# Loading x in single blocks between the gate weights, and x for the residual in four parts along the outputs

## The chip, the cores and the metric

One core of a Trainium2 chip (trn2) runs the whole kernel. The metric is device time in microseconds; the time of a kernel is the median of its runs. Five engines work side by side: TensorE (PE, with its weight loads as PEld), VectorE (DVE), ScalarE (ACT), GpSimd (POOL) and SyncE (SP), whose only work here is to issue DMAs, in the order of its instructions.

## The reference

x is 2048 tokens by 512 channels in bf16. It is normalised once, and two branches are added to it: attention in a sliding window, and a gated MLP that mixes over the tokens.

```python
xn = layernorm(x)
# A: 32 heads of 16 channels, causal, window of 256 keys
q, k, v = split(xn @ wqkv)
p = softmax(mask(q @ k.T * 16 ** -0.5))
A = (p @ v) @ wo
# B: Fh = 688
z = gelu(xn @ w_in)                       # 2048 x 1376
z1, z2 = z[:, :688], layernorm(z[:, 688:])
g = w_sp @ z2 + b_sp[:, None]             # w_sp is 2048 x 2048
B = (z1 * g) @ w_out
out = x + A + B
```

## The kernel before

The tokens are 16 blocks of 128 (`NB`). The work has two stages, and every order in it is written out by hand: each engine runs its instructions in the order in which the program emits them, and SP issues the DMAs in that order too, all on one queue. An instruction that waits holds up everything behind it on its engine.

**Stage one** (to about 56 us) makes, for each block n, the normalised and transposed x and the two gate halves:

- `load_x(n2)` (L189) loads two blocks of x, 2 x 128 rows, with one DMA (L196). Blocks 0 and 1 come as two DMAs (`split`, L194).
- `stats(n)` takes mean and variance on DVE (L254, L255), adds the epsilon (L119, `rs_v`) and has POOL raise to the power -0.5 (L120, `rstdx`).
- `norm(n)` (L260) makes `xn` on DVE; it needs the `rstdx` of POOL.
- `transpose_x(n)` transposes blocks 0 to 5 on PE (L274, tile `tp`) and copies to `xnT` on ACT (L277). From block 6 on a transposing DMA does it (L265).
- `do_z(n, half)` multiplies block n with one half of `w_in` (L285, 8 matmuls of 4 row chunks) into tile `zs`, and ACT applies the gelu (L293). Half 1 is z2, half 0 is z1.
- `load_win(half, c0, c1)` (L204) loads two of the four row chunks of one half of `w_in`, 344 KB.

SP's order at the start is: x blocks 0 and 1; half 1 of `w_in` in two parts; x blocks 2 and 3 in one DMA; x blocks 4 and 5; half 0 of `w_in` in two parts; then, after a small DVE write into `wqkv` (L326) which makes that load wait, x blocks 6 and 7, `wqkv` and the rest of x. PE's order is: warm-up matmuls on zeros, transpose(0), three more of those, transpose(1), `do_z(0, 1)`, `do_z(1, 1)`, transpose(2), `do_z(0, 0)`, transpose(3), `do_z(2, 1)`, and so on. DVE's is: stats(0), stats(1), norm(0), norm(1), stats(2), stats(3), norm(2), stats(4), norm(3), and so on.

**Stage two** follows the list `ORDER`, a string of tokens. `q` computes scores on PE (L479) and exponentials on ACT (L487); `m` masks (L498 on POOL, L503 on DVE); `a`, `A`, `B`, `C` multiply with v (`values`, L532, tile `o_t`, many short matmuls); `t` transposes the result (`oT`); `p`, `P` are projections from `xnT` (L135, L151); a number k is k mixer matmuls (L397, tile `gf`, two halves of 16 for each of 16 blocks, with `wspT` of that block loaded by a transposing DMA, L381, one block ahead). After each half DVE adds the bias and multiplies with z1 (L404). `o`, `O` are outputs in two parts for each block: four matmuls with `wo_sb` (L428), then six with `w_out_sb` (L434) whose weights `uT` are z1 transposed by a DMA (`load_uT`, L420, at most three blocks ahead of the output); DVE then adds the residual (L439) and a DMA writes the block out (L440).

The residual x is not kept from stage one. When the last projection has been emitted (`last_proj`), nothing reads `xnT` any more, and its space is filled with x again: four DMAs of 512 KB at one place (L583), of which the c-th brings blocks c, c + 4, c + 8 and c + 12. `xres[n]` is the residual of block n.

Of the kernel before, what the change touches and what calls it, by code (L numbers as in the profile page):

```python
# [8 lines left out]
P = 128  # L9
BF = mybir.dt.bfloat16  # L10
# [5 lines left out]
D = 512  # L16
# [5 lines left out]
NB = S_TOK // P  # L22
NDC = D // P
# [45 lines left out]
def kernel(  # L69
# [12 lines left out]
    nc = tc.nc  # L82
    x2 = A_x.flatten_outer_dims()
# [5 lines left out]
    xnT = pers.tile([P, NDC, S_TOK], BF, name="xnT")  # L89
# [27 lines left out]
    def rpow(dst, var, n):  # L117
        v = sml.tile([P, NB], F32, name="rs_v")
        nc.vector.tensor_scalar(out=v[:, :n], in0=var, scalar1=LN_EPS, scalar2=None, op0=ALU.add)  # L119
        nc.gpsimd.tensor_tensor(out=dst, in0=v[:, :n], in1=negh[:, :n], op=ALU.pow)  # L120
# [3 lines left out]
    def bank(name, ring):  # L124
        if ring:
            return ps_s.tile([P, 2, 512], F32, name=name, tag="S")[:, 0, :]
        return ps_y.tile([P, 512], F32, name=name, tag="y")[:]
# [50 lines left out]
    with tc.tile_pool(name="win_pool", bufs=1) as winp, tc.tile_pool(  # L178
        name="xsp", bufs=8
# [6 lines left out]
        make_identity(nc, ident[:])  # L186
        xs_tiles = {}

        def load_x(n2, split=False):  # L189
            xs = xsp.tile([P, 2, D], BF, name="xs")  # L190
            if split:
                for j in range(2):
                    r = (2 * n2 + j) * P
                    nc.sync.dma_start(out=xs[:, j, :], in_=x2[r : r + P, :])  # L194
            else:
                nc.sync.dma_start(  # L196
                    out=xs[:],
                    in_=x2[2 * n2 * P : (2 * n2 + 2) * P, :].rearrange("(j p) d -> p j d", p=P),
                )
            for j in range(2):  # L200
                xs_tiles[2 * n2 + j] = xs[:, j, :]

        def load_win(half, c0, c1):
            nc.sync.dma_start(  # L204
                out=w_in_sb[:, c0:c1, half * FH : (half + 1) * FH],
                in_=B_w_in[c0 * P : c1 * P, half * FH : (half + 1) * FH].rearrange(
                    "(c p) f -> p c f", p=P
                ),
            )

        load_x(0, split=True)
        load_win(1, 0, 2)
        load_win(1, 2, 4)
        load_x(1)
        warm = sml.tile([P, 1], F32, name="warm")
        nc.scalar.activation(out=warm[:], in_=esel[:, 0:1], func=ACT.Gelu_apprx_tanh)

        nc.gpsimd.affine_select(
            out=fmask[:], in_=fmask[:], pattern=[[-1, P]], compare_op=ALU.is_gt,
# [3 lines left out]
            out=esel[:], in_=esel[:], pattern=[[-32, 4]], compare_op=ALU.is_ge,  # L223
# [3 lines left out]
            out=esel[:], in_=esel[:], pattern=[[32, 4]], compare_op=ALU.is_ge,  # L227
# [24 lines left out]
        def stats(n):  # L252
            st = sml.tile([P, nc.vector.BN_STATS_DIM], F32, name="st")
            nc.vector.bn_stats(out=st[:], in_=xs_tiles[n])  # L254
            nc.vector.bn_aggr(out=mvx[:, n, :], in_=st[:])  # L255
            rpow(rstdx[:, n : n + 1], mvx[:, n, 1:2], 1)

        def norm(n):
            xn = xnp.tile([P, D], BF, name="xn")
            nc.vector.tensor_scalar(  # L260
                out=xn[:], in0=xs_tiles[n], scalar1=mvx[:, n, 0:1],
                scalar2=rstdx[:, n : n + 1], op0=ALU.subtract, op1=ALU.mult,
            )
            if n >= X_DMA:
                nc.sync.dma_start_transpose(out=xnT[:, :, n * P : (n + 1) * P], in_=xn[:])  # L265
            else:
                xn_tiles[n] = xn
# [11 lines left out]
        def do_z(n, half):  # L279
            zp2 = ps_s.tile([P, 2, 512], F32, name="zs", tag="S")  # L280
            zp = zp2[:].rearrange("p a q -> p (a q)")
            f0 = half * FH
            for c in range(NDC):
                for lo, hi in Z_RANGES:
                    nc.tensor.matmul(  # L285
                        zp[:, lo:hi],
                        lhsT=xnT[:, c, n * P : (n + 1) * P],
                        rhs=w_in_sb[:, c, f0 + lo : f0 + hi],
                        start=(c == 0),
                        stop=(c == NDC - 1),  # L290
                    )
            dst = z1_all if half == 0 else z2_all
            nc.scalar.activation(out=dst[:, n, 0:FH], in_=zp[:, 0:FH], func=ACT.Gelu_apprx_tanh)  # L293
# [28 lines left out]
        transpose_x(1)  # L322
        do_z(0, 1)
        stats(2)
        stats(3)
        nc.vector.memset(wqkv[0:1, 0, 0:1], 0.0)  # L326
        load_x(3)
        nc.sync.dma_start(out=wqkv[:], in_=A_wqkv.rearrange("(c p) f -> p c f", p=P))
        for n2 in range(4, NB // 2):
            load_x(n2)  # L330
        norm(2)
        do_z(1, 1)
        transpose_x(2)
        stats(4)
# [3 lines left out]
            out=emask[:, 0:1], in_=esel[:], op=ALU.add, axis=mybir.AxisListType.X  # L338
        )
        nc.vector.tensor_scalar(  # L340
            out=emask[:, 1:2], in0=emask[:, 0:1], scalar1=-1.0, scalar2=1.0,
# [74 lines left out]
    def load_uT():  # L416
        n = len(uT_tiles)
        if n < NB and n < NB - (len(g_steps) + 2 * NB - 1) // (2 * NB) and n <= max(out_n[0], 0) + 3 - (out_n[0] < 0):
            uT = utp.tile([P, NFC, P], BF, name="uT")
            nc.sync.dma_start_transpose(out=uT[:], in_=z1_all[:, n, :])  # L420
            uT_tiles[n] = uT
            load_uT()

    def out_part(n, fo, c0, c1, part):
        if part == 0:
            for G in range(NG):
                oT = oT_tiles[(G, n // 2)]
                nc.tensor.matmul(  # L428
                    fo[:, c0:c1], lhsT=oT[:, (n % 2) * P : (n % 2 + 1) * P],
                    rhs=wo_sb[:, G, c0:c1], start=(G == 0), stop=False,  # L430
                )
            return
        for c in range(NFC):
            nc.tensor.matmul(  # L434
                fo[:, c0:c1], lhsT=uT_tiles[n][:, c, :], rhs=w_out_sb[:, c, c0:c1],
                start=False, stop=(c == NFC - 1),
            )
        xr = xres[n][:, c0:c1]
        nc.vector.tensor_tensor(out=xr, in0=fo[:, c0:c1], in1=xr, op=ALU.add)  # L439
        (nc.scalar if n >= NB - 3 and c1 == D else nc.sync).dma_start(  # L440
            out=out2[n * P : (n + 1) * P, c0:c1], in_=xr
        )

    def output(ring):
        n, part = o_steps.pop(0)
        last = n == NB - 1
        if part == 0:
            out_n[0] = n
            load_uT()
            fo_tiles[n] = bank("fo", ring)  # L450
        out_part(n, fo_tiles[n], 0, D - LAST * last, part)
        if last and part == 1:
            fo = bank("fo", not ring)
            for part in range(2):
                out_part(n, fo, D - LAST, D, part)
# [38 lines left out]
    def masks(i):  # L494
        E = E_tiles[i]
        for j, (G, kb, qb) in enumerate(TILES[i]):
            if kb == qb:
                nc.gpsimd.affine_select(  # L498
                    out=E[:, :, j, :], in_=E[:, :, j, :], pattern=[[0, 8], [1, P]],
                    compare_op=ALU.is_ge, fill=0.0, base=0, channel_multiplier=-1,  # L500
                )
            elif qb == kb + 2:
                nc.vector.tensor_tensor(  # L503
                    out=E[:, :, j, :], in0=E[:, :, j, :],
                    in1=fmask[:].unsqueeze(1).to_broadcast([P, 8, P]), op=ALU.mult,
                )
# [55 lines left out]
    def finish():  # L562
# [9 lines left out]
        out=w_out_sb[:, 0:5, :], in_=B_w_out[0:640, :].rearrange("(c p) n -> p c n", p=P)  # L572
# [1 line left out]
    nc.sync.dma_start(out=w_out_sb[0 : FH - 5 * P, 5, :], in_=B_w_out[5 * P : FH, :])  # L574
    tokens = ORDER.split()
    last_proj = max(i for i, t in enumerate(tokens) if t[0] in "pP")
    xres = {}
    for i, t in enumerate(tokens):
        if i == last_proj + 1:
            for n in range(NB):  # L580
                xres[n] = xnT[:, n % NDC, (n // NDC) * D : (n // NDC + 1) * D]
            for c in range(NDC):
                nc.sync.dma_start(  # L583
                    out=xnT[:, c, :].rearrange("p (m d) -> p m d", d=D),
                    in_=x2.rearrange("(m c p) d -> c p m d", p=P, c=NDC)[c],
                )
        if t[0] == "q":
            scores(int(t[1:3]), int(t[3]))
        elif t[0] == "m":
            masks(int(t[1:3]))  # L590
        elif t[0] in "aABC":
            values(int(t[1]), int(t[2]), t[0])
        elif t[0] == "t":
            finish()
        elif t[0] in "pP":
            proj(t[1], int(t[2]), int(t[3]), ring=t[0] == "P")
        elif t[0] in "oO":
            output(t[0] == "O")
        else:
            for _ in range(int(t)):  # L600
                mix()
# [30 lines left out]
```

## Time and profile before

| | us |
|---|---|
| median of 3 timed runs | 266.06 (265.9 to 266.5) |
| the profiled execution, its own time | 267.51 |
| its span, first to last instruction | 265.8 |
| TensorE matmul busy | 256.3 |
| ScalarE busy | 205.6 |
| VectorE busy | 197.7 |
| GpSimd busy | 122.0 |

The timeline gives for each group of instructions its start in us from the start of the span, its length in us, engine, line, operation, out<-in, and how many were merged; in brackets stands the idle time of that engine just ahead and what ended it. The view of waits gives who waited for whom: us in total, times, longest. The DMA view gives for a stretch each queue's packets, MB, and the time that its packets took as a share of 16 engines; q1 is the queue of SP, q8 carries instructions. A landing time runs from the issue to the last byte. The granted clock of TensorE was 1.000 throughout.

### The profile page before, as it was taken

What the parts mean: (1) busy time and instruction counts of PE and PEld (TensorE: products, weight loads), DVE (VectorE), ACT (ScalarE), POOL (GpSimd) and SP (SyncE); (2) the same over time, 40 slices, a digit from 0 to 9 for tenths busy, and PEclk for the clock granted to TensorE, in tenths of its full rate; (3) what the DMA queues carried; (4) which work ended last, traced back from release to release, by engine and by line L of the source; (5) the groups of instructions that cost most, each with busy time, mean ns of one, the idle gap of its engine ahead of it and who ended that gap; (6) DMA issues with size and microseconds to landing.
All of it is one profiled execution on the core that took longest, in us unless ns stands there. A gap on an engine that the chain in (4) does not pass through costs nothing.

```text
span 265.8 us, 7432 instructions
## 1 busy us (share of the span) xinstructions
PE 256.3 (96%) x3166; PEld 143.1 (54%) x3199; DVE 197.7 (74%) x384; ACT 205.6 (77%) x233; POOL 122.0 (46%) x140
## 2 busy tenths in 40 slices
PE   7799999999999999999999999999998999999995
PEld 3465665654545555555575456655574454545543
DVE  4799999667687788788797778897868473686532
ACT  3577767689999999999988989988887986782000
POOL 4243445215442663758454556455468344365100
PEclk9999999999999999999999999999999999999999
DMA  6693122950405072230330323651369263434433
GB/s 212 217 337 62 39 42 59 169 180 2 109 2 112 0 111 22 62 81 2 79 81 2 79 44 41 72 52 40 81 194 226 60 131 77 73 82 71 118 78 83
DMA packets 61216, 23.83 MB, mean 90 GB/s; under 512 B 52304, under 2 KB 60672, under 8 KB 61184
## 3 DMA queue, kind: packets, MB, share of 16 engines
q1 hardware_dynamic: 60704, 23.06, 40.2%
q8 instruction: 25, 0.41, 0.7%
q10 hardware_dynamic: 432, 0.30, 0.4%
q0 software_dynamic: 48, 0.00, 0.3%
q14 instruction: 7, 0.06, 0.1%
HBM read 8.41 MB, written 2.10 MB: 40 GB/s over the span
## 4 chain that ended last, share of the span: by engine, by line
PE 93%; DMA 2%; DVE 1%; issue 1%; SPq 1%; DVEq 0%
PE gf L397 31%; PE zs L285 13%; PE S L479 12%; PE m L151 10%; PE o_t L532 8%; PE fo L434 8%; PE m L135 6%; PE fo L428 5%; DMA xs<-in_A_x_dram 2%; DVE st L254 0%; PE tp L274 0%; SPq L204 0%; DVE xnT L439 0%; SPq L194 0%; DVE o_c L548 0%
## 5 line engine op out<-in xcount | busy, mean ns | idle before, releaser
L487 ACT ACTIVATE E<-S 128x1024 bf16<-128x1024 f32 x180 | 168.9, 1043 | 17.9 <-PE S L479 9.1
L397 PE MATMUL gf<-z_all,wspT 128*128 128x344 bf16 x512 | 95.1, 311 | 1.0 <-issue 1.0
L498 POOL TENSOR_SCALAR_AFFINE_SELECT E<-E 128x1024 bf16<-128x1024 bf16 x64 | 79.2, 1259 | 32.4 <-ACT E L487 32.2
L397 PEld LDWEIGHTS <-wspT 128*128 128x128 bf16 x512 | 44.1, 98 | 36.9 <-issue 16.5
L503 DVE TENSOR_TENSOR E<-E,fmask 128x1024 bf16<-128x1024 bf16 x56 | 52.6, 967 | 2.6 <-ACT E L487 2.5
L554 POOL TENSOR_TENSOR o_norm<-o_c,rsum 128x256 bf16<-128x256 f32 x32 | 21.5, 671 | 62.0 <-DVE rsum L552 59.3
L285 PE MATMUL zs<-w_in_sb,xnT 128*128 128x512 bf16 (+1 forms) x249 | 39.1, 307 | 0.4
L479 PE MATMUL S<-q_ring,k 32*128 32x128 bf16 (+2 forms) x760 | 37.2, 267 | 0.0
L293 ACT ACTIVATE z_all<-zs 128x688 bf16<-128x688 f32 x32 | 23.8, 744 | 12.8 <-PE zs L285 12.8
L151 PE MATMUL m<-xnT,wqkv 128*128 128x512 bf16 x111 | 31.5, 380 | 1.0 <-issue 0.2
L285 PEld LDWEIGHTS <-xnT 128*128 128x128 bf16 x256 | 22.2, 98 | 14.9
L404 DVE SCALAR_TENSOR_TENSOR z_all<-gf,b_all,z_all 128x344 bf16<-128x344 f32 x32 | 18.2, 567 | 15.3 <-PE gf L397 15.3
L548 DVE STREAM_TRANSPOSE o_c<-o_t 128x512 f32<-128x512 f32 x32 | 22.3, 697 | 7.2 <-PE o_t L532 6.5
L479 PEld LDWEIGHTS <-k 32*128 32x128 bf16 x760 | 12.7, 92 | 25.9 <-issue 25.2
L439 DVE TENSOR_TENSOR xnT<-fo,xnT 128x512 bf16<-128x512 f32 (+2 forms) x17 | 11.2, 659 | 17.2 <-PE fo L434 17.2
L532 PE MATMUL o_t<-E,v 128*32 128x128 bf16 (+1 forms) x1080 | 23.4, 238 | 0.0
L434 PE MATMUL fo<-w_out_sb,uT 128*128 128x512 bf16 (+2 forms) x101 | 23.3, 366 | 0.1
L532 PEld LDWEIGHTS <-v 128*32 128x32 bf16 x1080 | 19.2, 97 | 5.1 <-issue 4.6
L120 POOL TENSOR_TENSOR rstdx<-rs_v,negh 128x1 f32<-128x1 f32 x16 | 10.3, 646 | 18.3 <-DVE rs_v L119 16.9
L171 DVE TENSOR_TENSOR k<-m,emask 128x1024 bf16<-128x1024 f32 x13 | 15.8, 1218 | 3.2 <-PE m L151 3.0
L151 PEld LDWEIGHTS <-wqkv 128*128 128x128 bf16 x128 | 11.7, 98 | 11.6 <-issue 1.7
L135 PE MATMUL m<-wqkv,xnT 128*128 128x128 bf16 x256 | 16.9, 219 | 0.2 <-DVE o_c L548 0.2
(51 smaller groups left out, 173.2 us busy)
## 6 DMA issues: line engine op xcount, KB each, us to landing
xnT<-in_A_x_dram SPq DMA_DIRECT2D x4, 512.0 KB, 5.6
xs<-in_A_x_dram SPq DMA_DIRECT2D x7, 256.0 KB, 6.7
out_dram<-xnT SPq DMA_DIRECT2D x13, 128.0 KB, 1.7
wqkv<-in_A_wqkv_dram SPq DMA_DIRECT2D x1, 1536.0 KB, 6.3
w_in_sb<-in_B_w_in_dram SPq DMA_DIRECT2D x4, 344.0 KB, 4.8
w_out_sb<-in_B_w_out_dram SPq DMA_DIRECT2D x1, 640.0 KB, 6.2
wo_sb<-in_A_wo_dram SPq DMA_DIRECT2D x1, 512.0 KB, 5.1
xs<-in_A_x_dram SPq DMA_DIRECT2D x2, 128.0 KB, 2.0
```

The source lines that it names most:

```text
L135: nc.tensor.matmul(m[:, j * P : (j + 1) * P], lhsT=xnT[:, c, n * P : (n + 1) * P], rhs=wqkv[:, c, 2 * D + G * P : 2 * D + (G + 1) * P], st ...
L151: nc.tensor.matmul(m, lhsT=wqkv[:, c, w0 : w0 + P], rhs=xnT[:, c, grp * 512 : (grp + 1) * 512], start=(c == 0), stop=(c == NDC - 1),)
L285: nc.tensor.matmul(zp[:, lo:hi], lhsT=xnT[:, c, n * P : (n + 1) * P], rhs=w_in_sb[:, c, f0 + lo : f0 + hi], start=(c == 0), stop=(c == NDC ...
L293: nc.scalar.activation(out=dst[:, n, 0:FH], in_=zp[:, 0:FH], func=ACT.Gelu_apprx_tanh)
L397: nc.tensor.matmul(gf[:, 0:FQ], lhsT=wsp_tiles[n][:, c, :], rhs=z2_all[:, c, lo : lo + FQ], start=(c == 0), stop=(c == NB - 1),)
L434: nc.tensor.matmul(fo[:, c0:c1], lhsT=uT_tiles[n][:, c, :], rhs=w_out_sb[:, c, c0:c1], start=False, stop=(c == NFC - 1),)
L479: nc.tensor.matmul(S[:, h2, j * P : (j + w) * P], lhsT=k_t[(G, kb // 4)][32 * s : 32 * s + 32, e, (kb % 4) * P : (kb % 4 + 1) * P], rhs=q_ ...
L487: nc.scalar.activation(out=E[:, j : j + 3 : 2, 0:nb, :].rearrange("p h b c -> p h (b c)"), in_=tiles[pr][:, :, 0 : nb * P], func=ACT.Exp, ...
L498: nc.gpsimd.affine_select(out=E[:, :, j, :], in_=E[:, :, j, :], pattern=[[0, 8], [1, P]], compare_op=ALU.is_ge, fill=0.0, base=0, channel_ ...
L503: nc.vector.tensor_tensor(out=E[:, :, j, :], in0=E[:, :, j, :], in1=fmask[:].unsqueeze(1).to_broadcast([P, 8, P]), op=ALU.mult,)
L532: nc.tensor.matmul(T[32 * s : 32 * s + 32, e, j * P : (j + l) * P], lhsT=v_t[(G, kb // 4)][:, kb % 4, s, e : e + 2, :].rearrange("p a d -> ...
L548: nc.vector.transpose(out=C[:, 0 : 32 * DH], in_=Tb)
```

## The change

Three things are changed.

1. At the start, blocks 2 and 3 of x become two DMAs. Block 2 is issued between the two parts of half 1 of `w_in`, block 3 behind the second part. SP has one DMA more to issue there.
2. On DVE, norm(2) is emitted ahead of stats(3) and no longer behind it (and behind the write into `wqkv`).
3. The residual x is loaded in four parts at four places. Part c holds blocks 4c to 4c + 3, in the same space `xnT[:, c, :]`. Part 0 is issued where all four were; part 1 when output 0 begins, part 2 when output 4 begins, part 3 when output 8 begins, each ahead of the `load_uT()` of that output. Number, size and row length of the DMAs are as before.

The order of instructions on PE, ACT and POOL is the same in both kernels.

```diff
-        def load_x(n2, split=False):
+        xs_pairs = {}
+
+        def load_block(n):
+            if n % 2 == 0:
+                xs_pairs[n // 2] = xsp.tile([P, 2, D], BF, name="xs")
+            xs_tiles[n] = xs_pairs[n // 2][:, n % 2, :]
+            nc.sync.dma_start(out=xs_tiles[n], in_=x2[n * P : (n + 1) * P, :])
...
-        load_x(0, split=True)
+        load_block(0)
+        load_block(1)
         load_win(1, 0, 2)
+        load_block(2)
         load_win(1, 2, 4)
-        load_x(1)
+        load_block(3)
...
         do_z(0, 1)
         stats(2)
+        norm(2)
         stats(3)
         nc.vector.memset(wqkv[0:1, 0, 0:1], 0.0)
         load_x(3)
...
-        norm(2)
         do_z(1, 1)
...
+    def load_xres(c):
+        part = xnT[:, c, :].rearrange("p (m d) -> p m d", d=D)
+        for m in range(4):
+            xres[4 * c + m] = part[:, m, :]
+        nc.sync.dma_start(
+            out=part, in_=x2[4 * c * P : (4 * c + 4) * P, :].rearrange("(m p) d -> p m d", p=P)
+        )
...
         if part == 0:
             out_n[0] = n
+            if n % 4 == 0 and n + 4 < NB:
+                load_xres(n // 4 + 1)
             load_uT()
...
         if i == last_proj + 1:
-            for n in range(NB):
-                xres[n] = xnT[:, n % NDC, (n // NDC) * D : (n // NDC + 1) * D]
-            for c in range(NDC):
-                nc.sync.dma_start(
-                    out=xnT[:, c, :].rearrange("p (m d) -> p m d", d=D),
-                    in_=x2.rearrange("(m c p) d -> c p m d", p=P, c=NDC)[c],
-                )
+            load_xres(0)
```

More of the change, by code (lines that the diff above doesn't have):

```diff
@@ L187, with load_x @@
         xs_tiles = {}
-        def load_x(n2, split=False):
-            xs = xsp.tile([P, 2, D], BF, name="xs")
[L191 to L198, printed above, removed]
-                )
+        xs_pairs = {}
[4 more added lines that the diff above has]
+            nc.sync.dma_start(out=xs_tiles[n], in_=x2[n * P : (n + 1) * P, :])
+        def load_x(n2):
+            xs = xsp.tile([P, 2, D], BF, name="xs")
+            nc.sync.dma_start(
+                out=xs[:],
+                in_=x2[2 * n2 * P : (2 * n2 + 2) * P, :].rearrange("(j p) d -> p j d", p=P),
+            )
             for j in range(2):
@@ L442, in out_part @@
         )
+    xres = {}
+    def load_xres(c):
+        part = xnT[:, c, :].rearrange("p (m d) -> p m d", d=D)
+        for m in range(4):
+            xres[4 * c + m] = part[:, m, :]
+        nc.sync.dma_start(
+            out=part, in_=x2[4 * c * P : (4 * c + 4) * P, :].rearrange("(m p) d -> p m d", p=P)
+        )
     def output(ring):
@@ L576 @@
     last_proj = max(i for i, t in enumerate(tokens) if t[0] in "pP")
-    xres = {}
     for i, t in enumerate(tokens):
         if i == last_proj + 1:
-            for n in range(NB):
-                xres[n] = xnT[:, n % NDC, (n // NDC) * D : (n // NDC + 1) * D]
-            for c in range(NDC):
-                nc.sync.dma_start(
-                    out=xnT[:, c, :].rearrange("p (m d) -> p m d", d=D),
-                    in_=x2.rearrange("(m c p) d -> c p m d", p=P, c=NDC)[c],
-                )
+            load_xres(0)
         if t[0] == "q":
```

## The prediction, made before the changed kernel ran

> **What bounds the kernel now.** I read the page first: busy times, then the chain that ended last.
>
> ```profile
> span 265.8 us, 7432 instructions
> ...
> PE 256.3 (96%) x3166; PEld 143.1 (54%) x3199; DVE 197.7 (74%) x384; ACT 205.6 (77%) x233; POOL 122.0 (46%) x140
> ...
> PE 93%; DMA 2%; DVE 1%; issue 1%; SPq 1%; DVEq 0%
> ```
>
> TensorE is busy in 256.3 of 265.8 us and is 93% of the chain. The change adds and removes no matmul, so it can only win idle time of TensorE. Where is that? The view of waits for PE names it; its other rows are TensorE's own start (1.3 us) and two of 0.2 us.
>
> ```profile
> PE tp L274 <- DVE xn L260: 2.0, 2, 1.8
> ...
> PE gf L397 <- issue: 1.0, 1, 1.0
> ```
>
> Two gaps are worth having: 1.8 us in which the transpose of a block of xn is not ready, and 1.0 us in a mixer matmul that waited for nothing the profile names. The change touches the place of each. Everything else follows TensorE: once a gap closes, the rest of the stream moves up as a whole, because between the gaps PE runs without one.
>
> **The first gap.** The timeline of the first 13 us:
>
> ```profile
> 2.71 0.99 SPq L196 DMA_DIRECT2D xs<-in_A_x_dram  x2
> ...
> 4.04 0.89 SPq L204 DMA_DIRECT2D w_in_sb<-in_B_w_in_dram  x2
> ...
> 5.79 0.41 DVE L260 TENSOR_SCALAR xn<-xs,mvx,rstdx 128x512 bf16<-128x512 bf16 x1 [0.46 <-POOL rstdx L120]
> ...
> 6.50 2.50 PE L285 MATMUL zs<-w_in_sb,xnT 128*128 128x512 bf16 x16
> ...
> 8.28 0.69 DVE L254 BATCH_NORM_STATS2 st<-xs 128x6 f32<-128x512 bf16 x1 [2.08 <-DMA xs<-in_A_x_dram]
> 9.01 0.18 DVE L255 BATCH_NORM_AGGREGATE mvx<-st 128x2 f32<-128x6 f32 x1
> ...
> 9.23 0.15 DVE L119 TENSOR_SCALAR rs_v<-mvx 128x1 f32<-128x1 f32 x1
> 9.30 0.68 DVE L254 BATCH_NORM_STATS2 st<-xs 128x6 f32<-128x512 bf16 x1
> 9.46 0.55 POOL L120 TENSOR_TENSOR rstdx<-rs_v,negh 128x1 f32<-128x1 f32 x1 [3.71 <-DVE rs_v L119]
> ...
> 10.31 0.41 DVE L260 TENSOR_SCALAR xn<-xs,mvx,rstdx 128x512 bf16<-128x512 bf16 x1
> ...
> 10.47 0.66 POOL L120 TENSOR_TENSOR rstdx<-rs_v,negh 128x1 f32<-128x1 f32 x1 [0.46 <-DVE wqkv L326]
> 10.64 0.69 DVE L254 BATCH_NORM_STATS2 st<-xs 128x6 f32<-128x512 bf16 x1
> 10.78 0.23 PEld L274 LDWEIGHTS <-xn 128*128 128x128 bf16 x4 [2.14 <-DVE xn L260]
> 10.78 0.40 PE L274 MATMUL tp<-ident,xn 128*128 128x128 bf16 x4 [1.79 <-DVE xn L260]
> ...
> 11.01 1.33 PE L285 MATMUL zs<-w_in_sb,xnT 128*128 128x512 bf16 x8
> ...
> 11.65 0.41 DVE L260 TENSOR_SCALAR xn<-xs,mvx,rstdx 128x512 bf16<-128x512 bf16 x1
> ...
> 12.18 0.39 PE L274 MATMUL tp<-ident,xn 128*128 128x128 bf16 x4
> ```
>
> PE ends the matmuls of blocks 0 and 1 at 9.00 (6.50 + 2.50) and stands until 10.78. Before that DVE stood 2.08 us for blocks 2 and 3 of x, issued at 2.71 behind both gate weights and there at 8.26. The queue is busy until then; the DMA view of 0 to 5.7, and of 0 to 8.26:
>
> ```profile
> q1 hardware_dynamic: 946, 1.08, 61.4%
> ```
>
> ```profile
> q1 hardware_dynamic: 1755, 2.00, 74.8%
> ```
>
> Ahead of and within that load lie x blocks 0 to 3 (0.52 MB) and two gate parts (0.70 MB), 1.23 MB in the queue's order, but 2.00 MB had moved when it counted as landed. At 0.36 MB/us (0.92 MB in 2.56 us) it landed 2.1 us later than its place in the order says: some of the 16 engines lag, and a load lands with its last packet.
>
> Step 1, block 2 moved up. Behind only blocks 0, 1 and one gate part it ends at 0.74 MB of the order instead of 1.23, which is about 4.8 us (0.34 MB before 5.7). DVE ends the norm of block 1 at 6.20 (5.79 + 0.41), so stats(2) starts at 6.20 instead of 8.28; with the same lag of 2.1 it would start at about 6.9. The statistics go on at the quoted steps: +0.73 aggregate, +0.22 rs_v, +0.23 POOL, which takes 0.55 to 0.66: rstd at 7.93 to 8.04, norm(2) to 8.49 at the latest. The transpose needs it at 9.00. **The 1.78 us gap closes, but not all of it is won.** What is late next?
>
> Step 2, norm(2) put ahead of stats(3). DVE now waits for POOL inside this chain (7.22 to about 8.0) with stats(3) queued behind the wait. From norm(2)'s start at about 8.05, stats(3) follows 0.33 later (10.31 to 10.64), so 8.38; its aggregate 0.72 and rs_v 0.21 give 9.31; stats(4) 0.15 behind it, again 0.72 and 0.22, and norm(3) about 0.08 after that: 10.48, its end 10.89, transpose(3) at 10.95. Before, transpose(3) ran at 12.18. So the DVE chain allows at most 12.18 - 10.95 = 1.23 us (0.5 to 0.6 if block 2 lags as above).
>
> Step 3, the other gate half. Between the two transposes lies do_z(0, 0), which reads the first half of w_in, issued at 4.04 and 4.49. The rows of tile w_in_sb say when such parts land:
>
> ```profile
> DMA to landing us min/median/max: 3.3/4.8/6.4
> ```
>
> The last issued has the longest, 4.49 + 6.4 = 10.89. The change leaves the bytes ahead of it as they are (2 blocks of x change places with a gate part) and adds one issue. Its second half of matmuls, 0.58 us (8 matmuls take 12.18 - 11.01 = 1.17), then begins at 10.89 and transpose(3) at 11.47: a gain of 12.18 - 11.47 = **0.71 us**. Bounds: 1.23 if that part lands early, about 0.3 if the added issue (0.45 us, from 0.89 for two) delays it in full. I take 0.71, as no byte ahead of it goes away. The second gate part, now behind 0.13 MB more, may also be late for do_z(0, 1); that only fills time in which do_z(0, 0) would have waited. The added issue and the extra waits on old transfers hide behind a queue full to 9 us.
>
> **The second gap.** Before, all of x for the residual (2 MB) is read in one burst after the last projection. SP's timeline, then PE's:
>
> ```profile
> 194.08 2.03 SPq L583 DMA_DIRECT2D xnT<-in_A_x_dram  x4
> 197.40 6.16 SPq L381 DMA_TRANSPOSE wspT<-in_B_w_sp_dram  x1
> ```
>
> ```profile
> 197.30 2.50 PE L532 MATMUL o_t<-E,v 128*32 128x128 bf16 x120
> ...
> 200.07 1.63 PE L397 MATMUL gf<-z_all,wspT 128*128 128x344 bf16 x10
> 201.63 0.41 PE L479 MATMUL S<-q_ring,k 32*128 32x384 bf16 x8
> ...
> 203.02 0.61 PE L397 MATMUL gf<-z_all,wspT 128*128 128x344 bf16 x3 [0.98 <-issue]
> ```
>
> The stalled matmuls are the eleventh to thirteenth of their mixer block, so their weights and bank were there; nothing was awaited. What is left is the instruction stream. The page has it as queue 8, and the DMA view of 200 to 203.5 has one packet of it, after none in 197 to 200 (only the first row):
>
> ```profile
> q8 instruction: 25, 0.41, 0.7%
> ```
>
> ```profile
> q1 hardware_dynamic: 1103, 1.09, 109.5%
> ```
>
> ```profile
> q8 instruction: 1, 0.02, 2.0%
> ```
>
> 25 packets for TensorE's 6365 records are one of 16 KB per 255 instructions. The 120 short matmuls with their weight loads use up nearly one packet in 2.5 us, just while 16 engines are full with 1.09 MB in 3 us. I read the stall as a packet held up in that burst. The change reads 0.5 MB here instead of 2; at 364 GB/s (1.09 MB in 3 us) that is 1.4 us, over before the 120 matmuls begin. **Gain 0.98 us**, between 0.98 and 0.
>
> [...] No row here shows the moment at which the packet was asked for.
>
> The three later parts. Each is one issue of about 0.5 us (2.03 for four) on SP and 0.5 MB ahead of a uT transpose. The second is behind wspT, which no longer holds SP for 6.16 us. The third comes before the uT of block 7, the fourth before that of block 11. The chain shows when the first of these is used, and the timeline when it was issued:
>
> ```profile
> 224.46 1.96 SPq L420 DMA_TRANSPOSE uT<-z_all  x1
> ...
> 240.87 1.21 SPq L420 DMA_TRANSPOSE uT<-z_all  x1
> ```
>
> ```profile
> 227.92 1.44 PE o_t L532 x80
> ...
> 238.38 1.29 PE fo L434 x6
> 239.82 1.44 PE o_t L532 x80
> ```
>
> ```profile
> xnT<-in_A_x_dram SPq DMA_DIRECT2D x4, 512.0 KB, 5.6
> ```
>
> From 224.46 to 238.38 are 13.9 us, against 0.5 of issue and 5.6 us of landing (the median of the four that came together, so too much for one alone). Block 8's residual has longer still. Cost 0; without that cover it would be up to 1.4 us each.
>
> **The sum.** The profiled execution took 267.51 us; -0.71 - 0.98 makes 265.82. It is 1.45 us above the median of the timed runs, 266.06, so it may stall more than they do. The same terms from the median: 266.06 - 1.69 = **264.4 us**.
>
> **The rivals.**
> A, the forecast: 264.4 us, 0.50. Its own range is 263.8 (first term 1.23) to 264.9.
> B, only the first term: the stall at 202 stays, because the fetch is not held by the burst, or the unprofiled runs never had it. For it speaks the 1.45 us between profile and median. 266.06 - 0.71 = 265.4, chance 0.25. [...]
> C, only the second: the engines that lag hold block 2 or the gate parts as long as they did blocks 2 and 3, so DVE starts near 8.28 again. Against it: 0.49 MB less before block 2 has ended. 266.06 - 0.98 = 265.1, chance 0.08.
> D, the change does not do what it says: both gaps reappear under other names (do_z(0, 0) stands for w_in until 12, wspT and the second part starve PE at 202). 266.1, chance 0.09.
> E, slower: the loads at about 199, 224 and 241 each meet a run of o_t matmuls (120 at 197.30, 80 at 227.92, 80 at 239.82) and hold up an instruction packet for 0.98. The old stall stays and two come: 266.06 - 0.71 + 2 x 0.98 = 267.3. It decides once new stalls exceed what the start won. Against it: 80 matmuls use two thirds of a packet and 0.5 MB is gone in 1.4 us. Chance 0.08.
>
> **How the numbers follow.** About 0.2% (0.53 us) is what a measurement can tell from no change. A, B and C are faster; B lies only 0.18 beyond the bound, so 0.05 of it goes to no change: faster 0.78, same 0.14, slower 0.08. The range: down to 263.5, A's best 263.8 less the 0.3 by which the runs scatter; up to 265.7, which takes in most of B and leaves out D and E.
>
> **What would show it.** In the changed profile: DVE's first statistics of block 2 near 6.2; transpose(2) near 9.0; a wait for w_in in do_z(0, 0), with transpose(3) at about 11.5 (at 10.95 if norm(3) is what holds it); no row "gf <- issue" of 1 us; the issue of wspT near 2 us instead of 6.16; the last output some 1.7 us earlier. I am wrong if PE waits as long in the first 13 us, if the "issue" wait stays near 202, or if one appears near 228 or 240.

## The result, and the profile after

| | before | after |
|---|---|---|
| median, us | 266.47 (8 runs, 265.90 to 266.99) | 265.38 (8 runs, 265.21 to 265.83) |
| the profiled execution, us | 267.51 | 265.24 |
| its span, us | 265.8 | 263.5 |

The changed kernel takes 0.9962 of the time before (95% interval 0.995 to 0.9974): 1.09 us faster. The forecast was 264.4 us, 1.66 below the 266.06 that was known then, with a range of 263.5 to 265.7. Direction and range hold; the size does not: of 1.69 us forecast 1.09 came, and the median of the kernel before lay 0.41 higher with eight runs than with three. The two profiles (2.3 us apart in span) promise even more than the timed runs give. That gap is what the experiments are about.

The page of the changed kernel, and its view of PE's waits:

```profile
span 263.5 us, 7433 instructions
...
PE 256.9 (98%) x3166; PEld 143.4 (54%) x3199; DVE 197.9 (75%) x384; ACT 205.5 (78%) x233; POOL 122.0 (46%) x140
...
PE 97%; issue 1%; DVE 1%; DVEq 0%
```

```profile
PE warm_t L251 <- DVE zeros L183: 1.3, 1, 1.3
PE m L135 <- DVE o_c L565: 0.2, 1, 0.2
```

TensorE went from 93% of the chain to 97%, the DMA that was 2% of it is gone, and so are both rows on which the forecast was built: "tp <- xn" with 2.0 us and "gf <- issue" with 1.0. The timeline of the start:

```profile
6.20 0.69 DVE L259 BATCH_NORM_STATS2 st<-xs 128x6 f32<-128x512 bf16 x1
...
6.91 2.50 PE L290 MATMUL zs<-w_in_sb,xnT 128*128 128x512 bf16 x16
...
7.95 0.41 DVE L265 TENSOR_SCALAR xn<-xs,mvx,rstdx 128x512 bf16<-128x512 bf16 x1 [0.66 <-POOL rstdx L120]
...
9.25 0.39 PE L279 MATMUL tp<-ident,xn 128*128 128x128 bf16 x4
...
10.31 0.41 DVE L265 TENSOR_SCALAR xn<-xs,mvx,rstdx 128x512 bf16<-128x512 bf16 x1
...
10.77 0.23 PEld L279 LDWEIGHTS <-xn 128*128 128x128 bf16 x4 [0.33 <-DVE xn L265]
10.77 0.40 PE L279 MATMUL tp<-ident,xn 128*128 128x128 bf16 x4
```

DVE begins block 2 at 6.20, waits for POOL with norm(2) until 7.95 and ends norm(3) at 10.72, on which the weight load of transpose(3) at 10.77 waits (0.33 us; PE itself loses about 0.13, as the eight matmuls ahead take 1.17). In the first profile transpose(3) was at 12.18, so between these two executions the start wins 1.41 us. The w_in parts land earlier than in the first profile (the longest took 6.4 us there):

```profile
DMA to landing us min/median/max: 3.3/4.2/5.1
```

At the second place, PE and SP:

```profile
195.91 2.50 PE L549 MATMUL o_t<-E,v 128*32 128x128 bf16 x120
...
200.25 0.41 PE L496 MATMUL S<-q_ring,k 32*128 32x384 bf16 x8
200.59 0.61 PE L402 MATMUL gf<-z_all,wspT 128*128 128x344 bf16 x3
```

```profile
192.69 0.38 SPq L455 DMA_DIRECT2D xnT<-in_A_x_dram  x1
196.01 2.33 SPq L386 DMA_TRANSPOSE wspT<-in_B_w_sp_dram  x1
```

The mixer matmuls follow the scores with no gap, and SP is held for 2.33 us by wspT instead of 6.16.

### The profile page after: what moved, and what is told of

Same layout as the page of the kernel before. It is cut to its first block, busy times and chain, and to the rows that moved or that the text cites. A ratio compares the mean times of both kernels' runs of the same rounds, so it can differ in the third digit from the quotient of the medians.

```text
span 263.5 us, 7433 instructions
## 1 busy us (share of the span) xinstructions
PE 256.9 (98%) x3166; PEld 143.4 (54%) x3199; DVE 197.9 (75%) x384; ACT 205.5 (78%) x233; POOL 122.0 (46%) x140
## 4 chain that ended last, share of the span: by engine, by line
PE 97%; issue 1%; DVE 1%; DVEq 0%
PE gf L402 31%; PE zs L290 14%; PE S L496 12%; PE m L151 10%; PE o_t L549 8%; PE fo L439 8%; PE m L135 6%; PE fo L433 5%; PE warm_t L251 2%; PE tp L279 1%; DVE xnT L444 0%; DVE o_c L565 0%; DVE zeros L183 0%; DVEq L565 0%
## 5 line engine op out<-in xcount | busy, mean ns | idle before, releaser
L120 POOL TENSOR_TENSOR rstdx<-rs_v,negh 128x1 f32<-128x1 f32 x16 | 10.2, 640 | 17.0 <-DVE rs_v L119 14.5
## 6 DMA issues: line engine op xcount, KB each, us to landing
xs<-in_A_x_dram SPq DMA_DIRECT2D x6, 256.0 KB, 6.8
```

## Experiments

**e1, the kernel before once more, unchanged.** The profile from which the forecast was read took 267.51 us, more than any of the 8 timed runs of that kernel. Of the 27 runs of it that were taken beside e1 to e4, three are about as slow (267.26 to 267.63).

> The kernel before, unchanged, to see how its executions differ. Theory 1 (the forecast): the instruction stall near 202 us belongs to every execution, so its profile shows the row 'gf <- issue' with about 1.0 us again and its spans lie near 265.8. Theory 2: that stall was in the one profiled execution and in few others; the spans lie near 264.7 (the median 266.47 less the 1.74 us that lie outside the span in the changed kernel's runs), spread over more than 0.5 us, and a profile without the stall has a span about 1.0 shorter.

Measured: 266.44 us (11 runs), ratio 0.9997 (0.9985 to 1.0008); the profiled execution took 266.51, span 264.7. Its waits of PE, and its start:

```profile
PE gf L397 <- issue: 1.1, 1, 1.1
PE tp L274 <- DVE xn L260: 0.8, 2, 0.5
```

```profile
7.14 0.69 DVE L254 BATCH_NORM_STATS2 st<-xs 128x6 f32<-128x512 bf16 x1 [0.83 <-DMA xs<-in_A_x_dram]
...
9.63 0.34 PE L274 MATMUL tp<-ident,xn 128*128 128x128 bf16 x3 [0.53 <-DVE xn L260]
```

Each of the two theories is half right. The spans are those of theory 2, but what the first profile had in excess was not the instruction stall, which is here again with 1.1 us. It was the first gap: blocks 2 and 3 of x are there at 7.14 instead of 8.28, and PE waits 0.5 us instead of 1.8.

**e2 and e3, one part of the change each.**

```diff
 e2, against the full change:
-            if n % 4 == 0 and n + 4 < NB:
-                load_xres(n // 4 + 1)
...
-            load_xres(0)
+            (the four loads at one place, as before)

 e3, against the kernel before:
+            if n % 4 == 0 and n + 4 < NB:
+                load_xres(n // 4 + 1)
...
-            (the four loads at one place)
+            load_xres(0)
```

> Only the start is changed (single loads of blocks 2 and 3, norm(2) ahead of stats(3)); x for the residual comes in one burst as before. Theory 1: it wins the start term alone and keeps the stall, so about 1 us slower than the full change (near 266.4). Theory 2: it is as fast as the full change within 0.3 us (near 265.4), and transpose(3) is near 10.8 in its profile.

> Only the residual load is changed (four parts along the outputs); the start is as before. Theory 1: 0.98 us faster than before (near 265.5). Theory 2: within 0.4 us of before (266.1 to 266.5), with less spread, since only those executions gain that had the stall; no row 'gf <- issue' of 1 us.

Measured: e2 266.43 us (12 runs), ratio 0.9999 (0.9989 to 1.001); e3 265.13 us (6 runs), ratio 0.995 (0.9932 to 0.9967). The whole gain is the residual load's, and the start brings nothing that can be seen: by e2's interval it is worth at most 0.3 us, so 0.71 is ruled out. The stall stays in e2 and goes in e3, as theory 1 says, and it is in the median; theory 2 is wrong. e2's profile:

```profile
PE gf L402 <- issue: 1.0, 1, 1.0
```

```profile
10.68 0.40 PE L279 MATMUL tp<-ident,xn 128*128 128x128 bf16 x4 [0.22 <-DVE emask L342]
```

and e3's, with the start as before:

```profile
PE tp L274 <- DVE xn L260: 0.5, 2, 0.3
```

```profile
6.86 0.69 DVE L254 BATCH_NORM_STATS2 st<-xs 128x6 f32<-128x512 bf16 x1 [0.53 <-DMA xs<-in_A_x_dram]
...
10.76 0.39 PE L274 MATMUL tp<-ident,xn 128*128 128x128 bf16 x4
```

With the old start transpose(3) is at 10.76, with the new one at 10.68 and (full change) 10.77. The wait for x has gone and another has come in its place: e2's row names `emask`, the small instruction behind norm(3) on DVE, but norm(3) itself ends at 10.62, just ahead of transpose(3).

**e4, norm(2) back where it was.** Part of what takes the place of the wait is the new order of DVE, which puts norm(3) late; this run undoes it.

```diff
         stats(2)
-        norm(2)
         stats(3)
...
+        norm(2)
         do_z(1, 1)
```

> The full change without the move of norm(2): DVE runs stats(2), stats(3), norm(2), stats(4), norm(3) as before. By the durations of the changed profile norm(2) then ends at about 8.65 instead of 8.36, still ahead of PE (9.25), and norm(3) at about 10.0 instead of 10.72, so PE does not wait for transpose(3): 0.13 us faster than the full change where the clock rises as late as in its profile, up to 0.5 faster where it rises early. Rival: stats(3) waits for block 3 behind the second gate part, norm(2) comes later than PE's 9.25, and it is slower than the full change by 0.1 to 0.5 us.

Measured: 265.61 us (10 runs, 264.75 to 265.71), ratio 0.9958 (0.9943 to 0.9973). The expected gain did not come in the median; three of the ten runs lie at 264.75 to 265.28, and whether these are the early rises of the expectation is not shown. In its profile neither xn(2) nor xn(3) is late; PE is:

```profile
5.96 1.31 PE L251 MATMUL warm_t<-zeros 128*128 128x512 bf16 x3
...
7.10 0.39 PE L279 MATMUL tp<-ident,xn 128*128 128x128 bf16 x4
```

```profile
11.13 0.38 PE L279 MATMUL tp<-ident,xn 128*128 128x128 bf16 x4
```

The three warm-up matmuls between the transposes run 0.43 us apart here, at half the pace that e1 has at the same point (1.31 us for the three, against 0.81 there), and push transpose(1) from 6.38 to 7.10.

**e5, e6 and e11, without those three matmuls.** e5 is the full change, e6 also has norm(2) back, e11 is e6 once more.

```diff
-N_WARM = (10, 3)
+N_WARM = (10, 0)
```

> The full change without the three warm-up matmuls between transpose(0) and transpose(1). Theory 3: the start term is lost because PE's own path, which before hid behind the wait for blocks 2 and 3, is now the late one, and it is longer where the clock rises late (zs began at 6.5 to 7.3 in the profiles so far, with the rise at 4.5 to 6.8). Without the three matmuls (0.81 to 1.31 us) transpose(1) follows xn(1) at 6.3 to 6.4 and transpose(2) is at 8.9 to 9.0 or earlier, but norm(3) holds transpose(3) at 10.7, so 0 to 0.2 us faster than the full change. Rival 3: PE stands between the transposes, the clock rises later still, more gate matmuls run at the slow rate, and it is 0.3 us slower or more.

> The same with norm(2) where it was. Theory 3: now neither the warm-up nor norm(3) holds PE; transpose(3) at 10.2 to 10.5, 0.3 to 0.6 us faster than the full change (264.8 to 265.1). Rival 3: slower than the full change, as the clock rises later.

> The full change with norm(2) back and without the three warm-up matmuls between the transposes, the version whose profile had no wait of PE on norm(3): theory 3 says 0.1 to 0.4 us faster than the full change and than the residual load alone; the rival, that the start has nothing left to give, says within 0.15 us of both.

Measured: e5 265.45 us (5 runs), ratio 0.9961 (0.9948 to 0.9975); e6 265.22 (5 runs), 0.9958 (0.9945 to 0.9972); e11 265.12 (5 runs), 0.9955 (0.9943 to 0.9968). e5 is level with the full change, at the edge of theory 3's band, and norm(3) holds transpose(3) at 10.78, as theory 3 says. e6 came 0.1 us above its band, and transpose(3) was at 10.63, not 10.2 to 10.5. e11 is 0.32 faster than the full change and 0.26 faster than the residual load alone on the same chip (e9, e10 below), which agrees with theory 3, but the intervals overlap, and e12, with the old start and without the three matmuls, is only 0.09 slower: most of the 0.26 may come from taking out the warm-up, and that the start adds anything is not shown.

e11's own profile is no clean start either. Block 3 comes late, as e4's rival had it, and do_z(0, 0) stands from 10.27 to 10.57 between its halves, for the second part of w_in as far as the landing times tell (the longest took 5.8 us); transpose(3) is at 11.15.

```profile
7.95 0.69 DVE L259 BATCH_NORM_STATS2 st<-xs 128x6 f32<-128x512 bf16 x1 [0.57 <-DMA xs<-in_A_x_dram]
```

**e7 and e8, the size of the burst.** e7 adds two loads behind the four, into `wqkv`, which nothing reads any more; e8 is e3 with the first two parts together.

```diff
 e7, against the kernel before, behind the four loads:
+            spare = wqkv[:].rearrange("p c f -> p (c f)")
+            for c in range(2):
+                nc.sync.dma_start(
+                    out=spare[:, c * S_TOK : (c + 1) * S_TOK].rearrange("p (m d) -> p m d", d=D),
+                    in_=x2.rearrange("(m c p) d -> c p m d", p=P, c=NDC)[c],
+                )

 e8, against e3:
             load_xres(0)
+            load_xres(1)
...
-            if n % 4 == 0 and n + 4 < NB:
+            if n in (4, 8):
```

> The kernel before with two more 512 KB loads of x behind the four, into space that nothing reads any more: the burst is 3 MB. Theory 4: the instruction packet waits until the loads issued ahead of it have drained on its engine; the burst ends 2.9 us later (1.05 MB at 0.364 MB/us), so the row 'gf <- issue' grows from 1.1 to about 4 us and the run is about 3 us slower than before. Rival 4: the engine takes packets of both queues in turn; the stall comes from the 120 short matmuls using up the stream while any burst runs, stays near 1.1 us, and the time stays within 0.5 us of before unless another wait appears (uT or wspT behind the burst, told by its own row).

> Only the residual load is changed as in the full change, but its first two parts come together at the first place: a burst of 1 MB; the start is as before. Theory 4: the burst ends at about 198, the instruction packet comes in time, no row 'gf <- issue', and the time is that of the kernel with four single parts (265.1 within 0.3). Rival 4: the burst still runs when the 120 matmuls begin at about 196, so the stall of about 1 us stays.

Measured: e7 266.68 us (8 runs), ratio 1.0003 (0.9993 to 1.0013); e8 265.41 (5 runs), 0.996 (0.9947 to 0.9974). e7's waits, its SP, and the DMA view of 199 to 200:

```profile
PE gf L397 <- issue: 1.3, 1, 1.3
```

```profile
197.00 8.43 SPq L381 DMA_TRANSPOSE wspT<-in_B_w_sp_dram  x1
```

```profile
q1 hardware_dynamic: 337, 0.34, 104.8%
q8 instruction: 1, 0.02, 7.0%
```

The burst lasts longer (SP is held 8.43 us instead of 6.3), the stall does not: 1.3 us, not 4. The packet comes in the middle of the burst, between 199 and 200, as in e1 with its 2 MB:

```profile
q1 hardware_dynamic: 335, 0.34, 103.8%
q8 instruction: 1, 0.02, 7.2%
```

In e3, with half a megabyte, the view of 196 to 197 has the packet and no load at all beside it:

```profile
q8 instruction: 1, 0.02, 6.1%
```

PE stands at the same point of its program in the three (the 120 matmuls begin at 195.9 to 196.2). So in these runs the burst delayed the packet by about 3 us, 2 MB (e1) and 3 MB (e7) alike, and the burst did not have to drain: in e7 q1 is still at 104.8% beside it. The end of the stall follows the packet: the packet ends at 201.71, 200.69, 200.22 and 200.77 in the first profile, e1, e2 and e7, and the stalled matmul begins at 203.02, 202.05, 201.56 and 202.09, each time 1.3 us later, though the stall itself varies from 0.98 to 1.30. Rival 4 is right about e7: its time is within 0.5 us of before. Theory 4 is wrong on the queue and right on e8: 1 MB is through by about 198, there is no "issue" row of 1 us, and its time is 0.28 above e3's, on another chip. In e8 the packet comes at 197.29, 1 us later than in e3, and that costs nothing yet.

**e9, e10 and e12, the start term sized directly.** The full change and the residual load alone, and the latter without the three warm-up matmuls, all on one chip; the edits are those above.

> The full change again, on one chip with the residual load alone, to size the start term between them. Theory 3 (the start is worth little because in most executions blocks 2 and 3 land near 7.1, not 8.3, the wait of PE is 0.3 to 0.5 us, and norm(3) and PE's own path take most of that): within 0.3 us of the residual load alone. Forecast's theory: 0.7 us faster than it.

> The residual load alone again: about 1.2 us faster than before (265.1 to 265.4). Theory 3: within 0.3 us of the full change. Forecast's theory: 0.7 us slower than the full change.

> The residual load alone with the start as before, but without the three warm-up matmuls. Theory 3: they lie ahead of a wait of 0.3 to 0.5 us for blocks 2 and 3, so taking them out changes nothing (within 0.15 us of the residual load alone) and only the wait grows by what PE saves. Rival: PE's path decides here too, and it is 0.3 us faster, or, if the clock then rises later, slower.

Measured: e9 265.44 us (265.30 to 265.57, 5 runs), ratio 0.9963 (0.9951 to 0.9976); e10 265.38 (265.14 to 265.45, 5 runs), 0.9962 (0.9948 to 0.9976); e12 265.21 (5 runs), 0.9956 (0.9944 to 0.9969). The start is worth 265.38 - 265.44 = -0.06 us, and 0.01 by e1 and e2, which is nothing within the scatter of 0.3. In the profiles e9 shows how it is lost, e10 what it would have replaced:

```profile
7.31 2.50 PE L290 MATMUL zs<-w_in_sb,xnT 128*128 128x512 bf16 x16
...
11.12 0.38 PE L279 MATMUL tp<-ident,xn 128*128 128x128 bf16 x4
```

```profile
9.42 0.40 PE L274 MATMUL tp<-ident,xn 128*128 128x128 bf16 x4 [0.30 <-DVE xn L260]
...
10.82 0.39 PE L274 MATMUL tp<-ident,xn 128*128 128x128 bf16 x4
```

e9 never waits for x, yet its gate matmuls begin only at 7.31 (6.50 in the first profile), because the warm-up ahead ran at half pace until 6.96, and PE's own path takes it to 11.12. e10 waits 0.30 us for x and is at 10.82. e12 lies 0.17 below e10, just outside its band of 0.15 but within their scatter.

## Why the prediction was right or wrong

- **Which gaps would close: right.** Stats(2) at 6.20, the transpose of block 2 no longer waiting, no "gf <- issue" row, wspT issued in 2.33 us, and no new stall at 222 to 241, where the later parts go.
- **The second gap, 0.98 us: right, and a little small.** e3 wins 1.35 us and e10 1.12, and the stall that goes measured 1.0 to 1.3 in every profile with the burst (first profile, e1, e2, e7). That it is the instruction stream is shown as far as this: the packet moves from 199 to 200 back to 196 to 197 when the burst shrinks, the stall goes with it, and PE goes on 1.3 us after the packet has ended in all four profiles that have the stall. The reason given was only half right: the packet came about 3 us later beside the burst (e1 and e7 against e3), but not only once the burst had drained, for 3 MB (e7) held it no longer than 2 MB (e1). By what mechanism a burst holds it is not shown.
- **The first gap, 0.71 us: this step failed.** Its bounds were 0.3 and 1.23; it measured -0.06 (e9 against e10) and 0.01 (e2 against e1). The gap closes as the forecast says; what was mis-sized is the gap. Three things in its working were wrong.
  First, its start. The 8.28 at which blocks 2 and 3 arrived belonged to that one execution, and so did the 6.4 us of w_in (at most 5.2 in the five others with the old start and all the warm-up); why its loads were late is open. In five other profiles with the old start and all 13 warm-up matmuls (e1, e3, e7, e8, e10) DVE begins them at 7.14, 6.86, 7.03, 7.28 and 6.92, PE waits 0.23 to 0.53 us with transpose(2), not 1.79, and transpose(3) is at 11.04, 10.76, 10.92, 11.17 and 10.82, not 12.18. Measured from there the changed start (10.77, in e2 10.68, in e9 11.12) has 0.15 us to win, by the medians 10.92 and 10.77.
  Second, the 1.45 us by which the profiled execution exceeded the median. The forecast saw them and gave them to the instruction stall (rival B); about 1.1 of them (12.18 - 11.04) were the first gap. It then took both terms in full from the median.
  Third, what is late next. The forecast held w_in's second half (10.89) to be the bound; no w_in part took longer than 5.1 us in the profile after, and the bound was norm(3) (10.72 for its end, 10.89 by the forecast's step 2), or PE's own path, which the forecast held fixed at 9.00 for its end of block 1 and from which transpose(2) follows at 8.90 to 9.66 in the four profiles with the new start and all the warm-up. Only where loads were late (e11) does w_in bound it, as forecast.
- **The rivals.** By its gain C came nearest (only the second term, 0.98 us of the 1.09 measured; chance 0.08), by its mechanism not: block 2 did come early. B, at 0.25, had the wrong term missing; that its 265.4 is the time measured is luck, a term too small taken from a base too low, and it is because the range took in B that 265.38 lies within it. E did not occur.

PE's own path is also later with the new start because TensorE's faster pace (warm-up matmuls 0.21 us apart instead of 0.43) comes later in it. The trace records when the full clock is granted for the first time (last section); in us from the start of the span:

| profiles | old start | new start |
|---|---|---|
| before, after | 4.42 | 6.15 |
| e1, e3; e2, e4 | 4.55, 4.69 | 5.43, 6.95 |
| e7, e8; e5, e6 | 4.99, 6.19 | 6.53, 6.40 |
| e10, e12; e9, e11 | 4.16, 6.72 | 6.96, 7.15 |

In each row every new start lies behind every old one, an order that chance alone would give once in 432. With all the warm-up the gate matmuls (tile `zs`) begin at 6.62 with the old start and 7.11 with the new, by the medians: as much as the wait for x that was to be won. Why the rise is later is open: until 5.4 us PE runs the same ten matmuls in all fourteen. It is not all: without the three matmuls `zs` begins at 6.81 to 6.85 in either start, and the new one still wins nothing that can be seen (e12 against e11).

## What to carry to other kernels

Before costing a gap of a microsecond or two, see whether the profiled execution is a typical one: where it stands far above the median, one of its gaps is probably not in the median, and no term should be taken from the median before a second profile has shown which. A wait at the start can cover another path that is nearly as long, as here; list the second and third latest arrival before booking the wait. Here a burst of loads (2 MB, 3 MB in e7) stalled TensorE, which waited for none of them, for 1.0 to 1.3 us, as far as the runs show through its instruction stream; spreading it beside the work that uses it cost nothing here, as each part was issued early enough.

## What the runs showed of the hardware

TensorE's pace at the start differs between executions although PE begins its warm-up at 1.26 us in each. The ten warm-up matmuls of the first profile, of e1 and of the changed kernel:

```profile
1.26 3.88 PE L246 MATMUL warm_t<-zeros 128*128 128x512 bf16 x10 [1.26 <-DVE zeros L183]
```

```profile
1.26 3.94 PE L246 MATMUL warm_t<-zeros 128*128 128x512 bf16 x10 [1.26 <-DVE zeros L183]
```

```profile
1.26 4.45 PE L251 MATMUL warm_t<-zeros 128*128 128x512 bf16 x10 [1.26 <-DVE zeros L183]
```

They run 0.43 us apart at first and 0.21 later. The views give the granted clock as 0.999 to 1.000 over the whole span in these three, but the trace has no record of it before the change of pace: its first record begins at 4.42, 4.55 and 6.15 in them, at 6.95 and 6.96 in e4 and e9, and from 4.16 to 7.15 over all fourteen profiles. So the granted clock "1.000 throughout" of the first profile holds only from 4.42 on. The first records last 256.0, 259.4 or 262.8 us, in steps of 3.4; the moment at which they begin varies by 3 us, and what sets it is open. With the new start, where PE's waits have no row for x (the changed kernel, e4, e9), this spread goes on to transpose(3): it is at 10.77 with the rise at 6.15, and at 11.13 and 11.12 with the rise at 6.95 and 6.96; the profiled executions took 265.24, 265.60 and 265.57 us. With the old start the wait for x took up the late rise of e8: it came at 6.19, and PE still waited 0.30 us for x with transpose(2).
